# Attention and two feed-forward layers on one core: where the second layer's weights are converted

## The chip, the cores and the metric

The kernel runs on one core of a Trainium2 chip. The core has TensorE (PE) for matrix products, VectorE (DVE), ScalarE (ACT) and GpSimd (POOL) for elementwise work, and SyncE (SP), whose queue issues all transfers (DMA) of this kernel. Each engine works through its own instructions in order and waits for semaphores of the others. The metric is the device time of one execution in microseconds (us).

## The reference

```python
# q, k, v: 4 batches x 8 heads x 768 positions x 64, fp32
scores = scale * q @ k^T                     # keep: first 4 positions, or the last 128
a = softmax(where(keep, scores, -1e9)); x = a @ v        # -> x: 3072 tokens x 512
h = x @ w1_in                                # 512 -> 2048
x = (h - tanh(h)) @ w1_out                   # 2048 -> 512
out = relu(x @ w2_in) ** 2 @ w2_out          # 512 -> 2048 -> 512
```

Weights are given in 64-bit floats, x in fp32, and the result is fp32.

## The kernel before

Each fp32 number is split into a high and a low part, and each product is three matmuls (high by high, high by low, low by high). `split` does it: ACT makes the high part (L150), DVE or POOL the low part (L151). Weights come as 64-bit floats and are made single on the chip by `to_single`: one instruction of ACT (L132) and three of DVE (L133 to L135).

The first layer goes in 8 tiles of 384 tokens, and each tile in 16 chunks `fc` of 128 hidden units: first product (L455), tanh (L466), difference (L467), split into `gs` or a spare buffer (L150, L151), and second product (L487) into `acc`, one chunk late, in tile 7 two chunks late. Between the pieces of a chunk a hook is called at four places, q = 0 to 3; it puts in the attention of the next tile. Tile 7 has no next one. There the second layer is opened: x is loaded (L681), four sums (L690) and seven splits of it go to POOL, and DVE and ACT turn its w_in into seven operands (L648, L657, L658).

The second layer goes in 6 tiles of 512 tokens with 8 groups each. A group is two hidden chunks, as seven block products in place of eight: `first` does four of them, `rest` three, and between them stands the second product (L756) of the group before, in two halves. w_out is fetched (L618) chunk by chunk out of DRAM, from where the kernel put it, converted, earlier.

That earlier conversion is the matter here. It goes in 64 half chunks, 32 of w_in and 32 of w_out, all through one buffer `wos` (`bufs=1`): load (L583), conversion with a `w_bit` buffer, and then for w_in a store of `w_bit` (L590), for w_out a split back into `wos` by ACT and POOL, and a store of that (L595). The next load must wait for that store. Before, `early_step` is called in every place q = 3 of tiles 1 to 6: in tiles 1 and 2 each call converts a half chunk of w_in and then loads the next one; in tiles 3 to 6 a call at an even place loads a half chunk of w_out and the call at the odd place after it converts it.

The order of PE is written by hand. The order of the other engines and of SP comes out of a scheduler, from priorities, its own estimates and `issue_after` (not before this instruction), and each then works in that order.

Of the kernel before, what the change touches and what calls it, by code (L numbers as in the profile page):

```python
# [13 lines left out]
I32 = mybir.dt.int32  # L14
# [5 lines left out]
P = 128  # L20
B, H, S, D = 4, 8, 768, 64
DM, DFF = 512, 2048
KC = DM // P
FC = DFF // P
T = 384
NT = B * S // T
# [13 lines left out]
NP = 7  # L40
# [87 lines left out]
def to_single(c, raw, w):  # L128

    nc = c.nc  # L130
    lo, hi = raw[:, :, 0], raw[:, :, 1]
    nc.scalar.activation(hi.bitcast(F32), hi.bitcast(F32), AF.Copy, scale=2.0 ** -112)  # L132
    nc.vector.tensor_scalar(w, hi, 3, None, ALU.logical_shift_left)  # L133
    nc.vector.scalar_tensor_tensor(w, lo, 29, w, ALU.logical_shift_right, ALU.bitwise_or)  # L134
    nc.vector.scalar_tensor_tensor(w, hi, -2147483648, w, ALU.bitwise_and, ALU.bitwise_or)  # L135


def convert(c, raw, dst, lo_eng):

    w = c.sb.tile([P, DM], I32, tag="w_bit", name="w_bit", bufs=3)[:, : raw.shape[1]]  # L140
    to_single(c, raw, w)
    dst = dst()
    split(c, dst, w.bitcast(F32), lo_eng)
    return dst


def split(c, dst, src, lo_eng):

    nc = c.nc
    nc.scalar.activation(dst[:, 0, :], src, AF.Copy)  # L150
    lo_eng.tensor_tensor(dst[:, 1, :], src, dst[:, 0, :].bitcast(F32), ALU.subtract)  # L151


class Weights:


    def __init__(self, c, w_in, w_out):
        self.c, self.src, self.t = c, (w_in, w_out), [[None] * FC, [None] * FC]
# [8 lines left out]
    def convert(self, i, fc):  # L167
        self.t[i][fc] = convert(self.c, self.t[i][fc], lambda: slot(self.c, ("wi", "wo")[i], fc, F32R),
                                (self.c.nc.vector, self.c.nc.gpsimd)[i])
# [378 lines left out]
def pools(c, es):  # L548
    tc = c.tc
    c.wp = es.enter_context(tc.tile_pool(name="wp", bufs=1))  # L550
    c.xp = es.enter_context(tc.tile_pool(name="xp", bufs=1))
    c.fp = es.enter_context(tc.tile_pool(name="fp", bufs=1))
    c.ps = es.enter_context(tc.tile_pool(name="ps", bufs=1, space=PSUM))
    c.sb_es = es.enter_context(ExitStack())
    c.sb = c.sb_es.enter_context(tc.tile_pool(name="sb", bufs=1))
    c.spare = lambda fc: c.sb.tile([P, 3 * WN], F32R, tag="p", name="p", bufs=2)


# [7 lines left out]
class Second:  # L566


    def __init__(self, c):
        self.c = c  # L570
        self.slots = {}
        self.w = {}
        self.wo = {}
        self.x = {}
        self.xs = {}
        self.f = {}

# [5 lines left out]

    def convert_in(self, i):
        c, (fc, h) = self.c, divmod(i, 2)
        w = c.sb.tile([P, DM], I32, tag="w_bit", name="w_bit", bufs=3)[:, : DM // 2]
        to_single(c, self.early, w)
        c.nc.sync.dma_start(c.wi2[fc, :, ts(h, DM // 2)], w.bitcast(F32))  # L590

    def convert_out(self, i):
        c, (fc, h) = self.c, divmod(i, 2)
        t = convert(c, self.early, lambda: c.fp.tile([P, 2, DM // 2], F32R, tag="wos", name="wos", bufs=1), c.nc.gpsimd)
        c.nc.sync.dma_start(c.wo2[fc, :, :, ts(h, DM // 2)], t.bitcast(F32))  # L595

    def early_step(self, step):

        c = self.c
        with c.tc.issue_after(c.last_a.ins), c.tc.issue_after(c.last_d.ins):  # L600
            if step < 2 * FC:
                if step == 0:
                    self.load(c.w2_in, 0)
                self.convert_in(step)
                if step + 1 < 2 * FC:
                    self.load(c.w2_in, step + 1)
            elif step % 2 == 0:
                self.load(c.w2_out, step // 2 - FC)
            else:
                self.convert_out(step // 2 - FC)  # L610

    def fetch_out(self, fc):
        c, k = self.c, fc % 4
# [9 lines left out]
    def open(self):  # L623
        c = self.c
        c.l2 = c.sb_es.enter_context(c.tc.tile_pool(name="l2", bufs=1))
        c.spare = lambda fc: c.l2.tile([P, 2 * DM], F32R, tag=f"wos{2 + fc // 2 % 2}", name=f"wos{2 + fc // 2 % 2}", bufs=1)
        self.load_x(0)
        self.load_in(0)
        self.load_in(1)
        self.sum_x(0)  # L630
        for name in ORDER:
            self.split_x(0, name)
# [135 lines left out]
    def run(self, left):  # L768
        nj = B * S // T2
        half = (len(left) + 1) // 2  # L770
        before = left[:half], left[half:]
        for n in range(nj * NG):
            j, g = divmod(n, NG)
            s = self.first(j, g)
            if g == NG - 1 and j + 1 < nj:
                for name in ORDER[:4]:
                    self.split_x(j + 1, name)
            for m in before[0]:
                m()
            self.rest(j, g, s)  # L780
            if g == NG - 1 and j + 1 < nj:
                for name in ORDER[4:]:
                    self.split_x(j + 1, name)
            for m in before[1]:
                m()
            if n + 1 < nj * NG:
                for f in range(2):
                    self.fetch_out(2 * ((n + 1) % NG) + f)
            if j + 1 < nj:
                if g == 2:  # L790
                    self.load_x(j + 1)
                if g == 4:
                    self.sum_x(j + 1)
            before = [lambda j=j, g=g, s=s: self.second(j, g, s, 0)], [lambda j=j, g=g, s=s: self.second(j, g, s, 1)]
        for part in before:
            for m in part:
                m()


def banded(c):  # L800

    nc, tc = c.nc, c.tc
    with ExitStack() as es:
        pools(c, es)
        layers = [Weights(c, c.w1_in, c.w1_out)]
        heads = Heads(c, None)
        second = Second(c)
        loaded = 0

        def next_chunk():  # L810
            nonlocal loaded
            if loaded < 2 * FC:
                layers[0].load(loaded % 2, loaded // 2)
                loaded += 1

        heads.vsink = c.sb.tile([P, H + 1, D], F32, tag="v_k", name="v_k", bufs=1)
        nc.vector.memset(heads.vsink, 0.0)
        c.eps = c.const.tile([P, 1], F32, tag="eps", name="eps")
        nc.vector.memset(c.eps, 1.0e-9)
        for n in range(H):  # L820
            heads.load(n)
            if n == 1:
                nc.sync.dma_start(heads.vsink[:NS, :H, :], c.vs[0, :NS])
            if n in (3, 5, 7):
                next_chunk()
                next_chunk()
        heads.masks = band_masks(c)
        for pos in range(8 * H + OFF):
            heads.tick(pos)
        for fc in range(LEAD):  # L830
            for i in range(2):
                with tc.issue_after(heads.mark[2].ins), tc.issue_after(heads.markd[2].ins):
                    layers[0].convert(i, fc)

        def hook(l, j, fc, q):
            if j == 0 and q % 2 == 0:
                next_chunk()
            if j + 1 < NT:
                heads.tick(64 * (j + 1) + OFF + 4 * fc + q)
            f = fc + LEAD - (q == 1)  # L840
            if j == 0 and q % 2 == 1 and LEAD <= f < FC:
                with tc.issue_after(c.last_a.ins), tc.issue_after(c.last_d.ins), tc.issue_after(c.last_r.ins):
                    layers[0].convert(int(q == 1), f)
            if 1 <= j < NT - 1 and q == 3:
                second.early_step((j - 1) * FC + fc)
            if j == NT - 1:
                if fc == 0 and q == 0:
                    c.sb_es.close()
                    second.open()
                if q == 3:  # L850
                    with tc.issue_after(c.last_a.ins), tc.issue_after(c.last_d.ins):
                        second.before(fc)

        with tc.manual_schedule(engines={mybir.EngineType.PE}):
            second.run(ffn(c, layers, lambda l, j: heads.x[j], hook))
# [133 lines left out]
```

## Time and profile before

| what | value |
|---|---|
| median of 3 runs | 1279.56 us (1279.18 to 1281.78) |
| profiled execution | 1281.62 us, of which the span 1279.4 |
| PE busy | 1241.4 us, 97% of the span |
| PE weight loads | 1160.9 us, 91% |
| DVE busy | 824.8 us, 64% |
| ACT busy | 656.1 us, 51% |
| POOL busy | 356.3 us, 28% |
| mean granted TensorE clock | 0.997 |

The share of an engine is over the whole span; a single tile or group can have another limit. In rows of a timeline the first number is the start in us from the start of the span, the second the duration of the piece, then engine, line, operation, output <- input and number of instructions; in brackets stands how long the engine was idle before, and for what it waited. SPq is the queue of SP, and its rows are the issues of transfers.

### The profile page before, as it was taken

Reading aid. Unit: us, or ns where it says so; the run is one execution under the profiler, and the core shown is the slowest. Engines: PE = TensorE matmul, PEld = TensorE weight load, DVE = VectorE, ACT = ScalarE, POOL = GpSimd, SP = SyncE. Lnnn points to the kernel's source line nnn. Section 1 sums busy time; section 2 is a strip of 40 time slices with the busy share of each in tenths; the row PEclk is TensorE's granted clock in tenths of the full one; section 3 lists DMA queues with packets and bytes.
Section 4 is the critical chain, followed back from the end, with each engine's and each line's share of the span. In section 5 each row is a group of like instructions: output and inputs, shape, how many; then the busy total and the mean of one; then the engine's idle time right before and its main releaser. Section 6 shows DMA issues by size and latency. Waiting matters only on the chain.

```text
span 1279.4 us, 21220 instructions
## 1 busy us (share of the span) xinstructions
PE 1241.4 (97%) x7632; PEld 1160.9 (91%) x7632; DVE 824.8 (64%) x2012; ACT 656.1 (51%) x1714; POOL 356.3 (28%) x349
## 2 busy tenths in 40 slices
PE   7999999999899999999999999999999999999997
PEld 5788899988899999999999998999999999999996
DVE  7899777777776777767775775455464554554543
ACT  7887666756566777766774542232322322323221
POOL 0222323323233343434341402032230320323100
PEclk9999999999999999999999999999999999999999
DMA  9741144443333433333413233343253342533432
GB/s 364 269 169 45 66 132 129 126 129 119 95 119 109 133 114 99 123 106 109 133 50 123 63 113 124 99 142 122 99 165 99 100 165 99 165 101 105 137 103 87
DMA packets 67795, 158.27 MB, mean 124 GB/s; under 512 B 6864, under 2 KB 29392, under 8 KB 67680
## 3 DMA queue, kind: packets, MB, share of 16 engines
q1 hardware_dynamic: 67680, 156.82, 37.3%
q8 instruction: 62, 1.02, 0.3%
q14 instruction: 53, 0.43, 0.1%
HBM read 131.63 MB, written 25.17 MB: 123 GB/s over the span
## 4 chain that ended last, share of the span: by engine, by line
PE 75%; DVE 12%; DMA 6%; ACT 5%; issue 2%; POOL 0%; SPq 0%; ACTq 0%; DVEq 0%; POOLq 0%
PE acc L756 21%; PE acc L487 14%; PE ps_h L455 12%; DMA wos<-in_w_in_dram 5%; PE ps_h L705 5%; PE ps_v L705 5%; PE ps_t L705 5%; PE ps_s L705 3%; DVE w_bit L135 3%; DVE w_bit L134 2%; PE ps_t L322 2%; DVE w_bit L133 1%; PE ps_s L270 1%; DVE gs L151 1%; PE ps_s L271 1%
## 5 line engine op out<-in xcount | busy, mean ns | idle before, releaser
L487 PE MATMUL acc<-gs,wo 128*128 128x384 f32 x1440 | 297.7, 343 | 1.0 <-ACT gs L150 0.6
L455 PE MATMUL ps_h<-x,wi 128*128 128x384 f32 x1392 | 292.7, 345 | 2.9 <-DVE t L467 2.8
L487 PEld LDWEIGHTS acc<-gs,wo 128*128 128x128 f32 x1440 | 246.2, 188 | 3.8 <-ACT gs L150 1.0
L455 PEld LDWEIGHTS ps_h<-x,wi 128*128 128x128 f32 x1392 | 237.0, 189 | 7.5 <-DVE t L467 6.8
L150 ACT ACTIVATE x<-gs 128x256 fp32r<-128x256 f32 x144 | 55.0, 412 | 201.9 <-DVE gs L722 127.4
L756 PE MATMUL acc<-wos,x 128*128 128x512 f32 x576 | 139.5, 391 | 0.0
L151 POOL TENSOR_TENSOR x<-gs,x 128x256 fp32r<-128x256 f32 x48 | 35.7, 743 | 333.0 <-ACT x L150 333.0
L756 PEld LDWEIGHTS acc<-wos,x 128*128 128x128 f32 x576 | 105.2, 188 | 19.9
L467 DVE TENSOR_TENSOR t<-ps_h,t 128x384 f32<-128x384 f32 x116 | 64.6, 557 | 70.3 <-ACT t L466 70.1
L279 ACT ACTIVATE p<-p,nm 128x272 f32<-128x272 f32 (+1 forms) x168 | 83.7, 498 | 25.6 <-DVE nm L272 24.1
L219 POOL TENSOR_TENSOR k_l<-qkv,k_h 128x416 fp32r<-128x416 f32 (+1 forms) x48 | 60.7, 1264 | 114.9 <-ACT k_h L218 114.4
L272 DVE CUSTOM_DVE_ANT_0 p<-ps_s,m 128x272 f32<-128x272 f32 (+1 forms) x168 | 69.7, 415 | 30.2 <-PE ps_s L271 28.6
L151 DVE TENSOR_TENSOR gs<-t,gs 128x384 fp32r<-128x384 f32 x120 | 71.6, 596 | 13.0 <-ACT gs L150 12.8
L150 ACT ACTIVATE gs<-t 128x384 fp32r<-128x384 f32 x120 | 62.8, 523 | 32.8 <-DVE t L467 30.3
L756 PE MATMUL acc<-wo,x 128*128 128x512 f32 x288 | 73.8, 391 | 2.4 <-DMA wo<-wo 2.4
L756 PE MATMUL acc<-wi,x 128*128 128x512 f32 x288 | 73.7, 391 | 0.0
L151 POOL TENSOR_TENSOR wos<-w_bit,wos 128x256 fp32r<-128x256 f32 x32 | 23.6, 739 | 175.2 <-ACT wos L150 72.2
L151 POOL TENSOR_TENSOR xop<-xs,xop 128x512 fp32r<-128x512 f32 x42 | 58.1, 1414 | 35.6 <-ACT xop L150 35.6
L307 ACT ACTIVATE pt<-ps_t 128x384 fp32r<-128x384 f32 (+1 forms) x112 | 51.7, 462 | 29.0 <-PE ps_t L322 28.3
L292 DVE TENSOR_SCALAR p<-p,sm 128x128 f32<-128x128 f32 (+1 forms) x144 | 64.5, 473 | 1.9
L756 PEld LDWEIGHTS acc<-wo,x 128*128 128x128 f32 x288 | 52.5, 188 | 12.5 <-issue 2.6
L151 DVE TENSOR_TENSOR x<-gs,x 128x256 fp32r<-128x256 f32 x96 | 46.9, 529 | 22.9 <-ACT x L150 22.9
(187 smaller groups left out, 2512.4 us busy)
## 6 DMA issues: line engine op xcount, KB each, us to landing
wos<-wo SPq DMA_DIRECT2D x48, 512.0 KB, 4.0
qkv<-in_a_dram SPq DMA_DIRECT2D x32, 608.0 KB, 4.2
wi<-wo SPq DMA_DIRECT2D x24, 512.0 KB, 3.2
wo<-wo SPq DMA_DIRECT2D x24, 512.0 KB, 4.3
qkv<-in_a_dram SPq DMA_DIRECT2D x24, 504.0 KB, 3.9
wi<-in_w_in_dram SPq DMA_DIRECT2D x16, 512.0 KB, 9.5
wo<-in_w_out_dram SPq DMA_DIRECT2D x16, 512.0 KB, 8.8
wos<-in_w_in_dram SPq DMA_DIRECT2D x32, 256.0 KB, 2.9
```

The lines of the kernel that those rows point to most:

```text
L150: nc.scalar.activation(dst[:, 0, :], src, AF.Copy)
L151: lo_eng.tensor_tensor(dst[:, 1, :], src, dst[:, 0, :].bitcast(F32), ALU.subtract)
L219: nc.gpsimd.tensor_tensor(s.kl[:, :nk], s.k[:, :nk], s.kh[:, :nk].bitcast(F32), ALU.subtract)
L272: c.last_r = nc.vector.tensor_tensor_reduce(out=s.p[:, u, :w], in0=sc[:, :w], in1=self.masks[kind], op0=ALU.add, op1=ALU.min, scale=-SCALE ...
L279: self.mark[n] = nc.scalar.activation(s.p[:, u, :w], s.p[:, u, :w], AF.Exp, bias=s.nm[:, u : u + 1], scale=-1.0, accum_out=s.sm[:, u : u + 1])
L292: nc.vector.tensor_scalar(s.p[:, u, :w], s.p[:, u, :w], s.sm[:, u : u + 1], None, ALU.mult)
L307: nc.scalar.activation(hi, src, AF.Copy)
L455: nc.tensor.matmul(h[:, :T], w[:, a, kc, :], x[kc][:, b, :], start=(kc == 0 and i == 0), stop=(kc == KC - 1 and i == 2))
L467: c.last_d = nc.vector.tensor_tensor(t, h[:, :T], t, ALU.subtract)
L487: nc.tensor.matmul(acc[m][:, :T], w[:, a, ts(m, P)], gs[:, b, :], **st)
L705: self.c.nc.tensor.matmul(bank, w[:, a, kc, :], x[:, b, kc, :], start=start and kc == 0 and i == 0, stop=kc == 1 and i == 2, skip_group_ch ...
L756: nc.tensor.matmul(self.acc[2 * th + m], gs[:, b, ts(m, P)], w[:, a, :], start=(g == 0 and q == 0 and i == 0), stop=(g == NG - 1 and q == ...
```

## The change

One half chunk is converted at every second place of tiles 1 to 7: `early_load` at the even places, `early_convert` at the odd ones, 8 in a tile. w_in takes tiles 1 to 4, w_out half chunks 0 to 23 tiles 5 to 7; the last eight go into the loop over the groups of the second layer's first tile, up to two calls in a group. The `w_bit` buffer comes from the second layer's `xs` buffers once that layer is opened. In the second layer the next tile's x is loaded after group 4 instead of 2, and its sums are made after group 5 instead of 4. Everything else is the same.

```diff
 def convert(c, raw, dst, lo_eng):
-    w = c.sb.tile([P, DM], I32, tag="w_bit", name="w_bit", bufs=3)[:, : raw.shape[1]]
+    w = c.bits()[:, : raw.shape[1]]
...
+    c.bits = lambda: c.sb.tile([P, DM], I32, tag="w_bit", name="w_bit", bufs=3)
...
-    def early_step(self, step):
...
+    def early_load(self):
+        if self.done < 4 * FC:
+            self.load(*((self.c.w2_in, self.done) if self.done < 2 * FC else (self.c.w2_out, self.done - 2 * FC)))
+    def early_convert(self):
+        if self.done < 4 * FC:
+            if self.done < 2 * FC:
+                self.convert_in(self.done)
             else:
-                self.convert_out(step // 2 - FC)
+                self.convert_out(self.done - 2 * FC)
+            self.done += 1
...
     def open(self):
+        c.bits = lambda: c.l2.tile([P, DM], I32, tag="xs", name="xs", bufs=NP)
...
+            if j == 0:
+                for _ in range(2):
+                    self.early_load()
+                    self.early_convert()
             if j + 1 < nj:
-                if g == 2:
+                if g == 4:
                     self.load_x(j + 1)
-                if g == 4:
+                if g == 5:
                     self.sum_x(j + 1)
...
-            if 1 <= j < NT - 1 and q == 3:
-                second.early_step((j - 1) * FC + fc)
+            if j >= 1 and q == 3:
+                with tc.issue_after(c.last_a.ins), tc.issue_after(c.last_d.ins):
+                    (second.early_convert if fc % 2 else second.early_load)()
```

The lines of the changed kernel stand up to five further down: L583 is L585, L595 is L597, L648 is L649, L657 and L658 are L658 and L659, L681 is L682, L690 is L691.

ACT in tile 7, from the split of chunk 3 (`wos3`) to that of chunk 4 (`gs`); `wo1`, `wo0` and `wi1` take operands of the second layer. Before:

```order
L150 ACTIVATE wos3_8748<-t_8747 128x384
L657 ACTIVATE wo1_8774<-x_8603 128x256
L657 ACTIVATE wo0_8768<-xs_8759 128x2x256
L657 ACTIVATE wi1_8771<-xs_8760 128x2x256
L466 ACTIVATE t_8800<-ps_h_8787 128x384
L150 ACTIVATE gs_8801<-t_8800 128x384
L466 ACTIVATE t_8831<-ps_s_8818 128x384
```

And the same place of the changed kernel, where `wos_8563` is a half chunk just loaded and `wos_8601` its high part:

```order
L150 ACTIVATE wos3_8585<-t_8584 128x384
L658 ACTIVATE wo1_8620<-x_8427 128x256
L466 ACTIVATE t_8646<-ps_h_8633 128x384
L132 ACTIVATE wos_8563<-wos_8563 128x256
L150 ACTIVATE gs_8647<-t_8646 128x384
L658 ACTIVATE wo0_8614<-xs_8605 128x2x256
L150 ACTIVATE wos_8601<-xs_8596 128x256
L658 ACTIVATE wi1_8617<-xs_8606 128x2x256
L466 ACTIVATE t_8679<-ps_s_8666 128x384
```

The first step of a conversion now stands ahead of chunk 4's split, two operands of the second layer stand behind it, and the half chunk's own split is between them.

SP at the end of tile 7: `wi15`, `wo15` and `wos2` are the places of w_out chunks 0, 1 and 2 for the second layer, `xs` loads of the x of its second tile, `o` results of the first layer. Before:

```order
L618 DMA wi15_9295<-wo2_63 128x1024
L681 DMA xs_9615<-x2_61 128x2x256
L618 DMA wos2_9411<-wo2_63 128x1024
L681 DMA xs_9617<-x2_61 128x2x256
L681 DMA xs_9619<-x2_61 128x2x256
L681 DMA xs_9621<-x2_61 128x2x256
L505 DMA x2_61<-o_9399 128x384
L505 DMA x2_61<-o_9402 128x384
L618 DMA wo15_9297<-wo2_63 128x1024
```

And the changed kernel there, where `wos_9095`, `wos_9130` and `wos_9186` are half chunks in their one buffer:

```order
L618 DMA wi15_9207<-wo2_63 128x1024
L597 DMA wo2_63<-wos_9095 256x1x256
L618 DMA wos2_9323<-wo2_63 128x1024
L585 DMA wos_9130<-in_w2_out_dram 128x512
L597 DMA wo2_63<-wos_9186 256x1x256
L505 DMA x2_61<-o_9311 128x384
L618 DMA wo15_9209<-wo2_63 128x1024
```

The fetch of chunk 1 stands behind the last load and store of tile 7, and the loads of the next x are gone from here.

SP again, at the last groups of the second layer's first tile, in the changed kernel: the load and the store of the last half chunks, the fetches of w_out chunks 14 and 15 (`wos2`, `wos3`) and the x loads of the second tile.

```order
L585 DMA wos_9691<-in_w2_out_dram 128x512
L597 DMA wo2_63<-wos_9698 256x1x256
L618 DMA wos2_10018<-wo2_63 128x1024
L585 DMA wos_9702<-in_w2_out_dram 128x512
L682 DMA xs_9811<-x2_61 128x2x256
L682 DMA xs_9813<-x2_61 128x2x256
L682 DMA xs_9815<-x2_61 128x2x256
L597 DMA wo2_63<-wos_9709 256x1x256
L682 DMA xs_9817<-x2_61 128x2x256
L618 DMA wos3_10020<-wo2_63 128x1024
```

In the kernel before, this stretch of SP holds fetches of w_out alone; the x loads stand at the end of tile 7, as above.

## Rows read from the trace of the kernel before

**Rows 1.** Busy time by stretch, tiles 1, 2, 3, 4 and 7 of layer 1.

```profile
core 0: us, PE busy (x) PEld busy (x) DVE busy (x) ACT busy (x) POOL busy (x), PEclk, DMA share, GB/s
162.50:252.30 89.80, 87.70 (x540) 83.91 (x539) 68.35 (x195) 58.86 (x164) 27.68 (x28) 1.00 0.43 131
252.30:355.00 102.70, 93.52 (x575) 88.23 (x575) 75.54 (x196) 63.70 (x170) 31.14 (x30) 1.00 0.38 117
355.00:439.30 84.30, 84.30 (x540) 84.26 (x539) 59.34 (x170) 58.33 (x166) 32.33 (x35) 1.00 0.34 112
439.30:528.10 88.80, 88.80 (x576) 88.74 (x575) 63.74 (x172) 63.26 (x169) 35.84 (x38) 1.00 0.34 110
699.70:770.20 70.50, 69.52 (x410) 68.32 (x409) 52.44 (x106) 36.49 (x74) 18.79 (x15) 1.00 0.32 100
```

**Rows 2.** Waits of PE's weight loads, tiles 1 and 2: us in total, times, longest.

```profile
PEld ps_s L270 <- DVE nm L272: 9.5, 13, 1.9
PEld ps_v L377 <- DVE pts L309: 4.0, 3, 2.5
```

**Rows 3.** Waits of ACT, tiles 1 and 2.

```profile
ACT wos L132 <- DMA wos<-in_w_in_dram: 28.9, 31, 2.4
```

**Rows 4.** Timeline: a half chunk of w_out in tile 4, the last one before tile 7.

```profile
454.28 0.43 ACT L132 ACTIVATE wos<-wos 128x256 f32<-128x256 f32 x1
...
458.74 0.52 SPq L595 DMA_DIRECT2D wo<-wos  x1
...
461.30 0.33 SPq L583 DMA_DIRECT2D wos<-in_w_out_dram  x1
...
693.08 0.43 ACT L132 ACTIVATE wos<-wos 128x256 f32<-128x256 f32 x1
...
695.91 0.74 POOL L151 TENSOR_TENSOR wos<-w_bit,wos 128x256 fp32r<-128x256 f32 x1 [3.83 <-ACT wos L150]
...
696.67 0.53 SPq L595 DMA_DIRECT2D wo<-wos  x1
```

**Rows 5.** DMA issues: count, KB each, median us from issue to landing.

```profile
wo<-wo SPq DMA_DIRECT2D x24, 512.0 KB, 4.3
...
wos<-in_w_out_dram SPq DMA_DIRECT2D x32, 256.0 KB, 2.7
...
xs<-x SPq DMA_DIRECT2D x24, 256.0 KB, 5.5
```

**Rows 6.** Timeline of tile 7: POOL's x splits, DVE, and PE at chunks 4 and 8.

```profile
707.13 9.79 POOL L151 TENSOR_TENSOR xop<-xs,xop 128x512 fp32r<-128x512 f32 x7
...
715.70 1.50 DVE L648 TENSOR_TENSOR xs<-x,xs 128x256 f32<-128x256 f32 x1
...
721.35 2.19 PE L487 MATMUL acc<-gs,wo 128*128 128x384 f32 x11 [0.15 <-DVE gs L151]
...
722.35 0.42 DVE L648 TENSOR_TENSOR xs<-x,xs 128x256 f32<-128x256 f32 x1
...
737.94 2.24 PE L487 MATMUL acc<-gs,wo 128*128 128x384 f32 x12
```

**Rows 7.** Timeline: PE at the second layer's first accumulation.

```profile
775.42 1.61 PE L756 MATMUL acc<-wo,x 128*128 128x512 f32 x6 [2.39 <-DMA wo<-wo]
```

**Rows 8.** Timeline: end of the second layer's first tile, first group of the next.

```profile
834.56 1.68 SPq L618 DMA_DIRECT2D wos<-wo  x2
...
837.68 5.25 POOL L151 TENSOR_TENSOR xop<-xs,xop 128x512 fp32r<-128x512 f32 x4 [7.13 <-ACT xop L150]
...
848.40 0.88 PE L705 MATMUL ps_v<-xop,wo 128*128 128x256 f32 x6
```

**Rows 9.** Busy time by stretch (columns of rows 1): after the start, and around rows 7.

```profile
36.00:46.00 10.00, 7.68 (x38) 5.60 (x37) 7.94 (x19) 9.63 (x26) 3.56 (x4) 0.90 0.73 274
46.00:50.00 4.00, 4.00 (x21) 3.82 (x20) 2.87 (x6) 2.62 (x9) 0.68 (x1) 0.82 0.00 0
772.90:783.30 10.40, 8.01 (x46) 6.94 (x45) 4.81 (x12) 1.95 (x5) 0.74 (x1) 1.00 0.39 134
```

More of the change, by code (lines that the diff above doesn't have):

```diff
@@ L576, in __init__ @@
         self.f = {}
+        self.done = 0
     def load(self, src, i):
@@ L587, in convert_in @@
         c, (fc, h) = self.c, divmod(i, 2)
-        w = c.sb.tile([P, DM], I32, tag="w_bit", name="w_bit", bufs=3)[:, : DM // 2]
+        w = c.bits()[:, : DM // 2]
         to_single(c, self.early, w)
@@ L595, in convert_out @@
         c.nc.sync.dma_start(c.wo2[fc, :, :, ts(h, DM // 2)], t.bitcast(F32))
-    def early_step(self, step):
[L599 to L608, printed above, removed]
-            else:
-                self.convert_out(step // 2 - FC)
+    def early_load(self):
[5 more added lines that the diff above has]
+                self.convert_in(self.done)
+            else:
+                self.convert_out(self.done - 2 * FC)
+            self.done += 1
     def fetch_out(self, fc):
```

## The prediction

> **What bounds the kernel now.** Four views were read, in this order: the page's totals, the stretches by tile, the waits in the stretches that stand out, and the rows around every place where a converted half chunk goes in the changed kernel. The totals say that TensorE (PE) is busy nearly all of the span, so only time in which PE waits can be won, and any new wait of PE is lost at full price. The stretches by tile [rows 1] run from one tile's first result copy to the next. Tiles 1 and 3 hold the same matmuls (x540), and so do tiles 2 and 4 (x575 and x576), yet tile 1 takes 89.8 us against 84.3 and tile 2 takes 102.7 against 88.8. Tiles 3 and 4 have no idle PE at all. What tiles 1 and 2 have more of is conversions: a w_in half chunk at each of 16 places, where tiles 3 and 4 convert a w_out half chunk at every second place. The waits of tiles 1 and 2 [rows 2] are for the scores' maximum and for copies out of PSUM, both on VectorE (DVE). Behind them stands ScalarE (ACT): in 31 of the 32 places its L132 waits for the load of the half chunk, 28.9 us in all [rows 3], because that load is issued only when the half chunk before it has left the one buffer. ACT works in order, so softmax and tanh steps stand behind L132.
>
> From tile 7 on the same view shows 70.5 us with 1 us of idle PE; no half chunk is converted there, but POOL has seven splits of the second layer's x and DVE splits its w_in.
>
> **Tiles 1 to 6: gain.** The change halves the conversions of tiles 1 and 2 (8 each instead of 16), and issues each load a place ahead of its conversion. I take tile 1 to become as long as tile 3, and tile 2 as tile 4: 89.8 - 84.3 = 5.5 and 102.7 - 88.8 = 13.9, so -19.4 [rows 1]. What is hidden there afterwards (three DVE instructions, one of ACT) is hidden in tiles 3 and 4 by the same work already, and a w_in half chunk has no split on top. The gain could be less if some of the extra time belongs to attention itself; -10 is the other bound, about half. Tiles 3 to 6 stay at 8 half chunks each: nothing.
>
> **Tile 7: loss.** Here each half chunk goes through one buffer: load, L132 on ACT, three DVE instructions, a split on ACT and POOL, store, and only then the next load. In tile 4 [rows 4] that took 454.28 to 458.74 = 4.46 from L132 to store, then 2.56 to the next load; the last half chunk before tile 7 took 693.08 to 696.67 = 3.6 [rows 4]. With 2.7 for a load to land [rows 5] the cycle is 3.6 + 2.56 + 2.7 = 8.9 to 9.7 us; I take 9.1. PE does four chunks in 16.6 us (721.35 to 737.94, [rows 6]), 8.3 for two, so the buffer is slower than the places that it serves.
>
> First harm: POOL's split of tile 7's first half chunk stands behind seven xop splits, which end at 707.13 + 9.79 = 716.92 [rows 6]. With 0.74 for such a split [rows 4] it ends at 717.7; the next load can go at 717.7 + 2.56 = 720.2, and lands at 722.9. In the order of the changed kernel the L132 for that half chunk stands on ACT immediately ahead of the hi split of chunk 4, and on DVE three conversions and five w_in instructions stand ahead of chunk 4's lo split. L132 ends at 722.9 + 0.43 = 723.4; nine DVE instructions at 0.42 [rows 6] give 727.2. PE needed that lo split at 721.35 [rows 6]: 5.9 us late. Two conversions later L132 again stands ahead of a split: 727.2 + 2 x 9.1 = 745.4 against 737.94 [rows 6], 7.4 late. After that the order has L132 behind the split, and the delay only stays.
>
> Second harm: the fetch of w_out chunk 1 for the second layer's first accumulation. In before it was what PE waited for (2.39 us, [rows 7]), and it landed at 775.42. Now SP has load and store of tile 7's last half chunk ahead of it. The second conversion's L132 starts at 722.9; the eighth is six cycles on, 722.9 + 6 x 9.1 = 777.5; store after 4.0, then 0.5 for its issue, and 4.3 for the fetch [rows 5]: 786.3. Against 775.42 that is +10.9, and it contains the delays before it, since PE waits there anyway. Bounds: 7.4 (only the first harm), and +14.5 with the cycle at 9.7. I take +10.9.
>
> **Boundary of the second layer's tiles 0 and 1: loss.** The last eight half chunks go about one to a group. Within the groups before the last I cost them at nothing: L132 waits for loads there too, but PE uses what ACT, DVE and POOL make of a group only in the group after it; without that cover each would add its conversion, up to 4.5 us as in tile 4 [rows 4]. The end is different. In before the next tile's x loads and POOL sums were done by the end of tile 7; now the loads stand in SP's queue behind the load of the last half chunk, which stands behind the fetch of chunk 14, issued at 834.56 [rows 8]. So: that load at 834.9, landed at 837.6, split and store by about 841.6; the x loads at 835.3 to 836.3, landing 5.5 later [rows 5] at 841.8. Then POOL needs three sums, two splits, one sum, and two splits before the fourth product of the next tile can run: eight instructions at 1.31 (5.25 for four, [rows 8]) to 1.40 (9.79 for seven, [rows 6]); the second, since sums are among them: 841.8 + 11.2 = 853.0. PE wanted it at 848.40 [rows 8]: +4.6. Bounds 3.9 (all at 1.31) and 6.1 (a start 1.5 us later). Later tiles have a whole group between their loads and their sums, without half chunks: nothing.
>
> **Clock.** After idle stretches the granted clock fell in this trace: 0.90 over 10 us in which PE was busy for 7.68, and 0.82 over the 4 after that [rows 9], which cost 10 x 0.10 + 4 x 0.18 = 1.7 us. Around the wait of 2.39 us before the second layer's accumulation it stayed 1.00 [rows 9]. The changed kernel has three gaps of 3 to 5 us, at chunk 4, at the fetch and at the boundary. I count one of them with a fall: +1.7; bounds 0 and 5.1.
>
> The Trainium skill, "TensorE: Matmul & The Clock Gate", section "HAM oscillation — how this bites in real kernels", says that waits for transfers between bursts of matmuls bring the slow clock back each time; by it all three gaps would pay. The trace shows both outcomes [rows 9], and no run so far shows gaps of this size in the middle of dense work.
>
> **Sum.** -19.4 + 10.9 + 4.6 + 1.7 = -2.2 us, against the profiled execution's 1281.62 (span 1279.4 and 2.2 around it). That execution is 2.06 above the median of the runs, 1279.56, so I subtract from the median: 1277.4, rounded to 1277.5.
>
> **Rivals.**
> - *The blocks are covered* (faster). If the cycle in tile 7 is short, or L132's landing is earlier than I reckon, the two chunks by which the second matmul lags absorb the delay, and only some DVE work of tile 7 shows. For it: DVE is idle for 18 of tile 7's 70.5 us [rows 1]. Against: SP's order, which puts the fetch behind the store whatever DVE does. Price: -19.4 and some 3 left over: 1263. If only one of the two losses comes, it is 1267 to 1273.
> - *The one buffer's cycle* (slower). In tile 7 DVE's instructions took up to 1.50 us beside POOL's splits, 0.42 after them [rows 6], and ACT and DVE carry work that tile 4 doesn't have. Each 0.1 us on the cycle costs six times that at the fetch. At 10.3 instead of 9.1 it is +7.2: 1284.7. It decides from a cycle of about 9.9 on: (1282.1 - 1277.5) / 6 = 0.77 more. For it: the long DVE rows; against: POOL has nothing after its seven splits, and ends before most of the eight half chunks.
> - *The waits of tiles 1 and 2 are not the conversions'* (slower). Then they lose only half, -9.7, and the losses stand: 1287. Against: tiles 3 and 4 do the same attention with no idle PE [rows 1].
>
> **How the numbers follow.** A change of 0.2%, 2.6 us, is about what a measurement of this kernel can tell from none: 1277.0 to 1282.1. The forecast, a gain of tiles 1 and 2 that tile 7 and the boundary eat up, gets 0.40; its own range is 1273 to 1282 (0.16 below 1277.0, 0.24 within). The covered case gets 0.18 and one loss alone 0.10, both faster. The longer cycle gets 0.24 (0.20 slower, 0.04 within), the third rival 0.08. Faster: 0.16 + 0.18 + 0.10 = 0.44; same 0.28; slower 0.28. The range of 8 in 10 reaches from the covered case, 1262, to the longer cycle with part of the clock, 1286.
>
> **What would show it.** Tiles 1 and 2 at about 84 and 89 us, without PE waits for L272 and L309: the gain. ACT's L132 waiting for its load in tile 7 and PE waiting at chunks 4 and 8 for DVE's L151, then up to 5 us for the fetch of chunk 1: the first loss. PE waiting for POOL's xop splits in the second layer's ninth group: the second. The clock below 1.00 right after those gaps: the last term. The prediction is wrong if tile 7 keeps its 70.5 us, or if tile 2 stays over 95.

## The result, and the profile after

| | before | changed |
|---|---|---|
| median (6 runs each, side by side) | 1281.22 us | 1297.61 us |
| ratio | | 1.0121, interval 1.0109 to 1.0134 |
| span of the profiled execution | 1279.4 us | 1295.4 us |
| mean granted TensorE clock | 0.997 | 0.989 |

The change made the kernel slower by 1.2%, where a gain of 2 us was forecast. The two traces can be laid side by side at four places: the copy that ends a tile (L501), the first accumulation of the second layer (775.42 before, [rows 7]), the fourth product of its second tile (848.40, [rows 8]) and the end.

| stretch | before | after | difference | forecast |
|---|---|---|---|---|
| start to tile 1 | 162.5 | 161.6 | -0.9 | 0 |
| tile 1 | 89.8 | 84.3 | -5.5 | -5.5 |
| tile 2 | 102.7 | 88.8 | -13.9 | -13.9 |
| tiles 3 to 6 | 344.7 | 344.7 | 0 | 0 |
| start of tile 7 to the first accumulation | 75.7 | 96.4 | +20.7 | +10.9 |
| from there to the fourth product of the second tile | 73.0 | 85.4 | +12.4 | +4.6 |
| from there to the end | 431.0 | 434.2 | +3.2 | (clock 1.7) |

Busy time by stretch of the changed kernel, columns as in [rows 1]: tiles 1, 2, 3 and 7, which answer to those rows; then four short stretches of tile 7 and two at the second tile of layer 2.

```profile
161.60:245.90 84.30, 84.30 (x540) 84.26 (x539) 59.24 (x171) 55.05 (x158) 26.45 (x28) 1.00 0.33 103
245.90:334.70 88.80, 88.80 (x576) 88.73 (x575) 63.75 (x172) 59.94 (x161) 29.93 (x30) 1.00 0.32 99
334.70:419.00 84.30, 84.30 (x540) 84.27 (x539) 59.25 (x171) 54.99 (x158) 26.40 (x28) 1.00 0.33 103
679.40:770.90 91.50, 77.55 (x413) 74.18 (x412) 58.44 (x126) 40.98 (x91) 28.91 (x20) 0.93 0.34 107
...
688.50:694.50 6.00, 2.85 (x15) 2.27 (x14) 5.28 (x6) 2.81 (x7) 6.00 (x6) 0.98 0.00 0
694.50:698.00 3.50, 3.50 (x12) 3.50 (x13) 3.50 (x4) 1.21 (x3) 3.50 (x3) 0.54 0.00 0
703.00:711.00 8.00, 5.11 (x20) 4.53 (x19) 6.39 (x15) 4.51 (x10) 2.17 (x1) 0.81 0.27 74
755.00:766.00 11.00, 7.39 (x36) 7.18 (x35) 7.06 (x17) 4.19 (x10) 1.83 (x2) 0.69 0.51 167
847.00:857.00 10.00, 4.41 (x20) 3.38 (x19) 5.79 (x10) 5.46 (x13) 8.19 (x7) 0.88 0.56 189
857.00:867.00 10.00, 8.86 (x38) 7.76 (x38) 3.74 (x6) 1.78 (x4) 8.76 (x8) 0.60 0.14 58
```

Tiles 1 and 2 have no idle PE any more and are as long as tiles 3 and 4: the gain came to a tenth. Tile 7 is 21 us longer. PE idles there for 14 us (91.50 - 77.55) where it idled for 1, and most of the rest stands in the column PEclk: its matmuls are the same, but they take 77.55 us in place of 69.52, because after the waits the engine ran at the lower level (6.1 of these 8 us are found row by row below). In the second short stretch the granted clock is 0.54, which is close to 1.2 GHz all through; PE had been busy for 2.85 of the 6 us before it.

How the half chunks went through the one buffer in tile 7 shows in ACT's L132, by start, duration and what it waited for; first of the eight, then five of the others.

```profile
688.68 0.42 ACT L132 ACTIVATE wos<-wos 128x256 f32<-128x256 f32 x1
...
703.72 0.44 ACT L132 ACTIVATE wos<-wos 128x256 f32<-128x256 f32 x1 [7.73 <-DMA wos<-in_w_out_dram]
...
714.27 0.43 ACT L132 ACTIVATE wos<-wos 128x256 f32<-128x256 f32 x1 [4.70 <-DMA wos<-in_w_out_dram]
...
724.68 0.44 ACT L132 ACTIVATE wos<-wos 128x256 f32<-128x256 f32 x1 [0.62 <-DMA wos<-in_w_out_dram]
...
737.44 0.44 ACT L132 ACTIVATE wos<-wos 128x256 f32<-128x256 f32 x1 [3.71 <-DMA wos<-in_w_out_dram]
...
766.43 0.44 ACT L132 ACTIVATE wos<-wos 128x256 f32<-128x256 f32 x1 [1.56 <-DMA wos<-in_w_out_dram]
```

From the second on each L132 stands waiting for its load. From the second to the eighth it is 62.7 us, six cycles of 10.45, where the forecast had 9.1. One of the cycles in full (second to third half chunk), on DVE, POOL and SP:

```profile
704.19 0.29 DVE L133 TENSOR_SCALAR xs<-wos 128x256 int32<-128x256 int32 x1 [5.32 <-ACT wos L132]
...
705.41 0.42 DVE L135 SCALAR_TENSOR_TENSOR xs<-wos,xs 128x256 int32<-128x256 int32 x1
...
706.59 2.17 POOL L151 TENSOR_TENSOR wos<-xs,wos 128x256 fp32r<-128x256 f32 x1 [8.46 <-ACT wos L150]
707.01 0.55 DVE L151 TENSOR_TENSOR gs<-t,gs 128x384 fp32r<-128x384 f32 x1
...
708.08 0.55 DVE L467 TENSOR_TENSOR t<-ps_s,t 128x384 f32<-128x384 f32 x1
...
708.79 0.52 SPq L597 DMA_DIRECT2D wo<-wos  x1
...
711.31 0.33 SPq L585 DMA_DIRECT2D wos<-in_w_out_dram  x1
```

L132 to store is 5.07 us, store to load 2.52, load to L132 2.96. In this cycle the first part is the one that grew most: POOL's split takes 2.17 us where [rows 4] has 0.74, for the fourth half chunk even 3.19, and DVE puts steps of the w_in operands between L133 and L135. Over the six cycles L132 to store takes 28.5 us, where 9.1 a cycle leaves 23.0 for it, and load to L132 18.8, where six times 2.7 is 16.2: 5.5 and 2.6 us of the excess. POOL's split ends at 708.76, 0.68 us after the start of L467 (708.08), which takes one input out of PSUM; the DVE instructions that ran since the split began have both inputs in SBUF. Seven of tile 7's eight splits end 0.67 to 0.69 us after the start of such an instruction (L467, once L739). Chunk 4's low split (707.01) stands behind all of DVE's steps, as forecast. What PE sees of it, the waits of PE in tile 7 and then from there to 900 us (us in total, times, longest):

```profile
PE acc L487 <- DVE gs L151: 6.2, 4, 2.6
PE ps_v L706 <- DVE t L467: 3.6, 1, 3.6
PE acc L487 <- ACT gs L150: 2.0, 2, 1.7
PE acc L487 <- ACT wos L150: 1.8, 2, 1.0
...
PE ps_h L706 <- POOL xop L151: 4.3, 1, 4.3
PE acc L757 <- DMA wo<-wo: 1.5, 1, 1.5
PE ps_h L706 <- ACT xop L150: 1.3, 1, 1.3
PE ps_t L706 <- POOL xop L151: 1.1, 1, 1.1
```

Of the first four the three on L487 are the waits for splits at chunks 2, 4, 6, 8, 11 and 13, and the one on L706 is for the PSUM bank of chunk 15's first product. The wait for the fetch answers to [rows 7], those for `xop` to [rows 8]. The places of PE that matter most, in order of time:

```profile
692.42 0.45 PE L487 MATMUL acc<-gs,wo 128*128 128x384 f32 x1 [1.68 <-ACT gs L150]
694.34 3.70 PE L487 MATMUL acc<-gs,wo 128*128 128x384 f32 x11 [1.47 <-DVE gs L151]
...
707.62 3.64 PE L487 MATMUL acc<-gs,wo 128*128 128x384 f32 x11 [2.56 <-DVE gs L151]
...
760.55 1.65 PE L706 MATMUL ps_v<-xop,wo 128*128 128x256 f32 x6 [3.61 <-DVE t L467]
762.00 4.04 PE L487 MATMUL acc<-gs,wo 128*128 128x384 f32 x12
...
775.83 1.63 PE L757 MATMUL acc<-wo,x 128*128 128x512 f32 x6 [1.53 <-DMA wo<-wo]
...
855.90 1.44 PE L706 MATMUL ps_h<-xop,wi 128*128 128x256 f32 x5 [4.31 <-POOL xop L151]
857.14 1.48 PE L706 MATMUL ps_s<-xop,wo 128*128 128x256 f32 x6
...
862.49 4.07 PE L757 MATMUL acc<-wos,x 128*128 128x512 f32 x12
```

Eleven matmuls of chunk 4 took 2.19 us before [rows 6]; here the eleven after the wait take 3.64. Taking from each such row what the same matmuls take elsewhere gives 1.5 at 694.34, 1.4 at 707.62, 0.6 at chunk 11, 2.6 at 760.55 and 762.00, and 3.8 between 855.90 and 866.40: 9.9 us by the clock, where the forecast had 1.7.

### The profile page after: what moved, and what is told of

The parts are those of the page before. It is cut to its first block, busy times and chain, and to the rows that moved or that the text cites. A ratio compares the mean times of both kernels' runs of the same rounds, so it can differ in the third digit from the quotient of the medians.

```text
span 1295.4 us, 21207 instructions
## 1 busy us (share of the span) xinstructions
PE 1245.1 (96%) x7632; PEld 1169.6 (90%) x7632; DVE 819.0 (63%) x2012; ACT 651.2 (50%) x1714; POOL 360.3 (28%) x349
## 3 DMA queue, kind: packets, MB, share of 16 engines
q8 instruction: 62, 1.02, 0.3%
## 4 chain that ended last, share of the span: by engine, by line
PE 77%; DVE 8%; DMA 5%; ACT 3%; POOL 3%; issue 2%; SPq 0%; ACTq 0%; POOLq 0%; DVEq 0%
PE acc L757 18%; PE acc L487 16%; PE ps_h L455 16%; PE ps_v L706 5%; PE ps_t L706 5%; PE ps_h L706 5%; DMA wos<-in_w_out_dram 3%; PE ps_t L322 2%; PE ps_s L706 2%; DVE w_bit L134 2%; DVE w_bit L135 2%; DMA wo<-wos 2%; PE ps_s L271 1%; PE ps_s L270 1%; PE ps_v L363 1%
## 5 line engine op out<-in xcount | busy, mean ns | idle before, releaser
L487 PE MATMUL acc<-gs,wo 128*128 128x384 f32 x1440 | 302.8, 348 | 8.2 <-DVE gs L151 6.2
L487 PEld LDWEIGHTS acc<-gs,wo 128*128 128x128 f32 x1440 | 250.5, 191 | 11.9 <-DVE gs L151 7.4
L467 DVE TENSOR_TENSOR t<-ps_h,t 128x384 f32<-128x384 f32 x116 | 64.6, 557 | 68.4 <-ACT t L466 68.4
L309 DVE TENSOR_TENSOR pt<-ps_t,pt 128x384 fp32r<-128x384 f32 x96 | 50.1, 522 | 21.1 <-ACT pt L307 21.1
L757 PEld LDWEIGHTS acc<-wo,x 128*128 128x128 f32 x288 | 52.5, 188 | 11.6 <-issue 1.7
L151 DVE TENSOR_TENSOR x<-gs,x 128x256 fp32r<-128x256 f32 x96 | 46.8, 529 | 24.3 <-ACT x L150 24.1
```

Source lines behind the costliest of these rows:

```text
L467: c.last_d = nc.vector.tensor_tensor(t, h[:, :T], t, ALU.subtract)
L487: nc.tensor.matmul(acc[m][:, :T], w[:, a, ts(m, P)], gs[:, b, :], **st)
L757: nc.tensor.matmul(self.acc[2 * th + m], gs[:, b, ts(m, P)], w[:, a, :], start=(g == 0 and q == 0 and i == 0), stop=(g == NG - 1 and q == ...
```

## The experiments

After the two traces the theory was: the conversions of tile 7 and of the second layer's first tile cost PE time because each half chunk passes through one buffer, and the cycle of that buffer is longer than the places it serves. The rivals: the conversions' own work on ACT, DVE and POOL, beside tile 7's work on w_in; and the second layer's later x loads. All ratios are to the kernel before.

| run | what | median us | ratio (interval) |
|---|---|---|---|
| e1_none_late | no half chunks in tile 7 and layer 2 (16 left out) | 1262.4 | 0.9863 (0.9846 to 0.9879) |
| e2_tile7_alone | the last 8 left out | 1281.0 | 1.0009 (0.9996 to 1.0022) |
| e3_layer2_alone | tile 7's 8 left out | 1264.0 | 0.9872 (0.9856 to 0.9888) |
| e4_before_prefetch | before, loads a place ahead | 1276.9 | 0.9974 (0.9964 to 0.9984) |
| e5_raw_buffer | changed, own buffer for loads | 1269.1 | 0.9915 (0.9890 to 0.9940) |
| e6_x_loads_early | changed, x loads as before | 1296.3 | 1.0115 (1.0090 to 1.0141) |
| e7_skip_first | changed, 7 in tile 7, 9 after it | 1290.1 | 1.0072 (1.0046 to 1.0099) |
| e8_spread_early | none in tile 7, 56 in tiles 1 to 6 | 1271.5 | 0.9929 (0.9907 to 0.9952) |
| e9_late_eight | e5, last 8 tied to groups 1 to 4 | 1264.2 | 0.9876 (0.9857 to 0.9894) |
| e10_late_nine | e9, 7 in tile 7, 9 after it | 1267.1 | 0.9900 (0.9880 to 0.9920) |
| e11_split_on_dve | changed, low half on DVE | 1280.7 | 1.0007 (0.9993 to 1.0020) |

**Where the loss sits: e1, e2, e3.** The hook's condition is cut for tile 7, or the loop over groups, or the first of the two with the count moved on:

```diff
-            if j >= 1 and q == 3:
+            if 1 <= j < NT - 1 and q == 3:          # e1, e3
-            if j == 0:
+            if j < 0:                               # e1, e2: loop of layer 2
+            if j == NT - 1 and fc == 0 and q == 3:  # e3
+                second.done = 3 * FC + FC // 2
```

> The changed kernel with conversions in tiles 1 to 6 alone; the last 16 half chunks of w_out are left out, and the fetches take chunks that are there instead, the same bytes. If all that was lost comes from the conversions in tile 7 and in the second layer's first tile, this keeps the 20.3 us won up to the start of tile 7 and loses nothing: tile 7 back at 70.5 us, about 1281.2 - 20.3 = 1261, ratio 0.984. Rival: the later loads and sums of the second layer's x (groups 4 and 5 in place of 2 and 4) cost the wait at its second tile by themselves: then 4 to 10 us remain there, 1265 to 1271.

> The changed kernel without the eight conversions of the second layer's first tile (left out; fetches take chunks that are there). If tile 7 and the second layer lose independently, the 20.7 us from the start of tile 7 to the first accumulation stay and the rest goes: 1261 + 20.7 = 1282, ratio 1.000. If the delays feed each other (a delayed last half chunk of tile 7 holds up the fetches), less than 18 stay: under 1279.

> The changed kernel without the eight conversions of tile 7 (left out; fetches take chunks that are there); those of the second layer's first tile are done. If the two lose independently: 1261 + 15.3 = 1276, ratio 0.996, with PE waiting for POOL's xop splits at the second tile for 5 us or more. If the boundary was late only because everything before it was late, 1261 to 1266.

e1 came out as expected: tiles 1 to 6 bring the gain, tile 7 is back at 70.6 us, and the later x loads alone cost nothing. From e1 to e2 it is 18.5 us, a little under the 20.7 of the trace: e2 came out as its first case. e3 was the surprise, its second case: the last eight alone cost 1.5 us, within the intervals, and not 15. Their first load goes out at the start of tile 7, where the buffer is free, and the last one 52.5 us after the first accumulation, where the changed kernel has 67.1. Both together cost 33 us by the ratios and 35 by the medians, so 13 to 15 us are neither the one nor the other: they come when both are there and tile 7's half chunks push the last eight later.

**Where the gain came from: e4.** The kernel before, with loads into the `w_bit` buffers, so that one is under way while another is converted:

```diff
-        t = c.fp.tile([P, 2, DM // 2], I32, tag="wos", name="wos", bufs=1).rearrange("p a c -> p (a c)")
+        t = c.sb.tile([P, DM], I32, tag="w_bit", name="w_bit", bufs=3)
...
+                    self.load(c.w2_in, step + 1)
                 self.convert_in(step)
-                    self.load(c.w2_in, step + 1)
```

> The kernel before, with each half chunk loaded into a w_bit buffer in place of the one wos buffer, so that the load of a half chunk is issued a place ahead of its conversion; 16 conversions in tile 1 and in tile 2 as before, all done before tile 7. If the waits of tiles 1 and 2 came from ACT standing at L132 for its load, these go and tiles 1 and 2 fall to 84 to 87 and 89 to 93: 1262 to 1268, ratio 0.985 to 0.990. If they come from the work of 16 conversions on DVE and ACT, at most half goes: 1271 or more, ratio over 0.992.

ACT's wait for loads at L132 in tiles 1 and 2 is gone, 0.7 us in place of 28.9 [rows 3]:

```profile
ACT w_bit L132 <- DMA w_bit<-in_w_in_dram: 0.7, 1, 0.7
```

Tiles 1 and 2 are 85.0 and 94.9 us long, 4.8 and 7.8 shorter. Tile 1 still holds 16 conversions, so there the load's wait was 4.8 of the 5.5 us. Tile 2 holds only 12 now, and tile 3 has 11 where it had 8 and takes 91.2 us in place of 84.3. So of the 19.4 us at most 12.6 are the load's wait, and 5.7 are left when tile 3 is counted. The whole gains 3 us, which falls under the expectation's second case, by its time; the sum of the first missed tile 3. Why tile 2 falls behind even without the wait is not shown.

**The cycle of the buffer: e5 and e11.** In e5 the load from tile 7 on goes into a buffer of its own, so it waits for DVE's L135 of the half chunk before and no longer for that one's split and store. In e11 the buffer stays, and DVE makes the low half.

```diff
+        c.raw = lambda: c.l2.tile([P, DM], I32, tag="raw", name="raw", bufs=1)    # e5, in open()
-        t = c.fp.tile([P, 2, DM // 2], I32, tag="wos", ...)
+        t = c.raw()
...
-        t = convert(c, self.early, lambda: ..., c.nc.gpsimd)
+        t = convert(c, self.early, lambda: ..., c.lo)      # e11: c.lo = c.nc.vector from open() on
```

> The changed kernel with a buffer of its own for the loaded half chunk from tile 7 on, so that a load waits for the conversion before it and no longer for that one's split and store; nothing is left out. If the cycle of the one buffer (10 to 15 us a half chunk in the trace after) is what made tile 7 long, the waits at chunks 4 and 8 and at the end go, the collision of the first half chunk with POOL's xop splits stays: tile 7 at 75 to 79 us in place of 91.5, and with the last eight done earlier also less at the second tile: 1268 to 1275 in all, ratio 0.990 to 0.996. If the work of the conversions on ACT, DVE and POOL beside the w_in operands is the cause, tile 7 stays at 86 or more: 1288 to 1298.

> The changed kernel with the one buffer kept, and the low half of a half chunk's split made by DVE instead of POOL from tile 7 on; nothing is left out. POOL took 2.2 and 3.2 us for such a split in tile 7 where it took 0.74 in tile 4; DVE would take about 0.5. If that slow split is a main part of the cycle, each of the eight gets 1 to 2.4 us shorter, and 8 to 14 us come back: 1283 to 1289. If the cycle is set by load, store and DVE's own queue, a DVE with more in it gives nothing: 1294 to 1300.

Tile 7 of e5, and then its PE waits from the start of tile 7 to the first accumulation:

```profile
680.20:752.60 72.40, 70.04 (x415) 68.90 (x414) 61.17 (x132) 42.68 (x93) 29.61 (x21) 1.00 0.44 143
```

```profile
692.23 0.44 PE L487 MATMUL acc<-gs,wo 128*128 128x384 f32 x1 [0.72 <-ACT gs L150]
694.16 2.18 PE L487 MATMUL acc<-gs,wo 128*128 128x384 f32 x11 [1.49 <-DVE gs L151]
758.74 1.62 PE L759 MATMUL acc<-wo,x 128*128 128x512 f32 x3 [3.87 <-DMA wo<-wo]
```

With the same eight conversions in it and one of the last eight besides, and DVE even busier than in the changed kernel (61.17 against 58.44), tile 7 takes 72.4 us. Three of POOL's splits still take 2.83 to 3.17 us there, but no load waits for them. The waits at chunks 4 to 15 are gone and so is the one for POOL's xop splits at the second tile. That settles it for the cycle: the work of the conversions finds room in tile 7, the wait for the buffer doesn't. It was expected a little longer (75 to 79).

In e11 tile 7 takes 77.3 us, with a cycle of 9.6 (700.20 to 757.58 for six), by ACT's second and eighth L132:

```profile
700.20 0.43 ACT L132 ACTIVATE wos<-wos 128x256 f32<-128x256 f32 x1 [1.58 <-DMA wos<-in_w_out_dram]
...
757.58 0.42 ACT L132 ACTIVATE wos<-wos 128x256 f32<-128x256 f32 x1
```

Against the changed kernel that is 15 us by the ratios and 17 by the spans, more than the 8 to 14 expected. L132 to store takes 3.9 us in the mean, 4.75 in the changed kernel. So POOL's split was a main part of what made the cycle long, although it is one instruction of 0.74 us by [rows 4]. But e11 moves two things more. The first split no longer stands behind POOL's xop splits, so the second L132 comes 20.7 us after the start of the tile and not 24.3; and SP's order came out otherwise, with the fetch of w_out chunk 1 ahead of the eighth half chunk's store. What each of the three gave of the 15 to 17 us is not shown.

**The collision at the start: e7 and e10.** The first conversion of tile 7 goes, and the loop of the second layer takes one more; e10 is the same on e9.

```diff
-            if j >= 1 and q == 3:
+            if 1 <= j < NT and q == 3 and (j < NT - 1 or fc >= 2):
```

> The changed kernel with tile 7's first conversion moved to the end: seven in tile 7, from its chunk 2 on, nine in the second layer's first tile; nothing is left out. If the collision of the first half chunk with POOL's seven xop splits costs what PE shows at chunk 2 (3.2 us idle, 1.5 by the clock) and starts the chain late, tile 7 falls by 5 to 10 us to 82 to 86: 1287 to 1292. If the cycle alone sets tile 7, it falls by no more than 3, and the ninth half chunk makes the second tile later still: 1294 to 1302.

> e9_late_eight with tile 7's first conversion, the one beside POOL's seven xop splits, moved to the end as well (seven in tile 7, nine in the second layer's first tile); nothing is left out. If the 2.2 us that PE waits at tile 7's chunk 2 in e5_raw_buffer come from DVE's conversion steps slowed beside those splits, they go: 1263 to 1266, 2 us under e9_late_eight. Rival: the ninth half chunk brings the wait at the second layer's second tile back: not under e9_late_eight.

e7 is 6 to 8 us under the changed kernel and its tile 7 is 83.2 us long, the numbers of its first case, but hardly for the reason given there: the chain does not start earlier (second L132 25.9 us after the start of the tile), it is one half chunk shorter, and its cycle is 9.2 us, with POOL's splits at 0.74 to 1.11 beside other DVE instructions than before. e10 shows that the collision itself gives nothing back: PE's wait of 2.4 us at chunk 2 becomes 1.3 at chunk 3 and 0.9 at chunk 4. No wait comes at the second layer's second tile, but a new one near the end of its first, where ACT stands at L132 for 7.3 us for the ninth half chunk:

```profile
814.13 0.98 PE L708 MATMUL ps_h<-xop,wo 128*128 128x256 f32 x6 [2.11 <-ACT wi L721]
```

It is not faster than e9.

**The x loads: e6.** Groups 2 and 4 in place of 4 and 5:

```diff
-                if g == 4:
+                if g == 2:
                     self.load_x(j + 1)
-                if g == 5:
+                if g == 4:
                     self.sum_x(j + 1)
```

> The changed kernel with the second layer's x loaded after group 2 and summed after group 4, as before; nothing is left out. If the loss at the second layer's second tile came from x loads queued on SP behind the last half chunks, 5 to 10 us of it go: 1287 to 1292. If it came from POOL, whose sums still stand behind a split that follows the late groups, it stays: 1295 to 1299.

Nothing came back, as in the second case, but PE's longest wait at the second tile is now another, 3.7 us for the fetch of the last w_out chunk, which needs the last half chunk's store:

```profile
861.54 5.28 PE L757 MATMUL acc<-wos,x 128*128 128x512 f32 x12 [3.74 <-DMA wos<-wo]
```

When the eight are late, one or the other waits for them.

**Better versions: e8 and e9.** e8 converts w_in at two of three places of tiles 1 to 3 and w_out at every second place of tiles 4 to 6:

```diff
+            p = (j - 1) * FC + fc
+            if 0 <= p < 3 * FC and q == 3:
...
+                    if p % 3 < 2:
+                        second.early_convert()
+                        second.early_load()
...
```

> All 64 half chunks without any in tile 7: w_in at two of three places of tiles 1 to 3 (32), w_out at every second place of tiles 4 to 6 (24), the last eight in the second layer's first tile as in e3_layer2_alone, which cost 1.5 us there; nothing is left out. Between 8 conversions a tile (no waits) and 16 (5.5 and 13.9 us in tiles 1 and 2), 10 or 11 should cost 1 to 3 us a tile: 1264 + 3 to 9 = 1267 to 1273, ratio 0.990 to 0.995. Rival: any two conversions in neighbouring places wait for the load as before, and half of the old loss comes in three tiles: 1276 or more.

Tiles 1 to 3 are 86.1, 91.2 and 85.4 us long, 5.3 us over 84.3, 88.8 and 84.3 together. e9 is e5, with the last eight behind an instruction of `first` in groups 1 to 4, so that the fetch of w_out chunk 1 is no longer behind a store of theirs on SP:

```diff
-            if j == 0:
-                for _ in range(2):
+            if j == 0 and g >= 1:
+                with self.c.tc.issue_after(s.mark.ins):
+                    for _ in range(2):
...
```

> e5_raw_buffer with the last eight half chunks tied to the second layer's groups 1 to 4, two in a group, so that the fetch of w_out chunk 1 stands ahead of their loads and stores on SP; nothing is left out. If the wait of 3.9 us for that fetch in e5_raw_buffer, and the slow clock after it, came from the queue on SP, both go back to the 2.4 us of the kernel before: 1.5 idle and about 1.5 of clock less, 1265 to 1268, ratio 0.988 to 0.990. Rival: two half chunks in a group delay the group's own results and PE waits there: 1269 to 1275.

The wait for the fetch is 1.65 us in place of 3.87:

```profile
757.11 1.61 PE L759 MATMUL acc<-wo,x 128*128 128x512 f32 x6 [1.65 <-DMA wo<-wo]
```

The whole came out a little under the 1265 to 1268 expected. e9 is the fastest with nothing left out: 1.2% under the kernel before, and 2 us from e1, which leaves a quarter of the conversions out. Both its steps, the load's own buffer and the place of the last eight, were taken from the waits above.

## Why the prediction was wrong

By the spans the forecast is missed by 18.2 us: 9.8 from the start of tile 7 to the first accumulation, 7.8 from there to the second tile, 1.5 after it, less 0.9 won before tile 1. The mechanism of the losses was the forecast's; the size of the buffer's cycle, and what hangs on it, was not.

- **Tiles 1 to 6** were right, to 0.1 us in each tile: a tile with eight conversions was there to be read [rows 1]. The reason given, ACT at L132, holds for tile 1 (4.8 of 5.5 us in e4); for both tiles it is at most 12.6 of 19.4, and the rest stays open.
- **Tile 7 fails at its cycle of 9.1 us**, made up from rows of tile 4 and tile 6 [rows 4]. It measured 10.45, and over six cycles that is 8.1 of the 9.8 us by which the stretch was missed. The start was 1.1 us late: the second L132 came 24.3 us after the start of the tile, forecast 23.2. In the cycle, L132 to store was the part most under-sized, 3.84 us of the 9.1 against 4.75 measured; the landing of the load, 2.7 against 3.1, is a third of the miss. The cycle was my rival on the slower side, priced at 10.3, with a chance of 0.24; what I held against it was that POOL has nothing to do after its seven splits. But idle before the split is not alone during it: three of the eight splits took 2.2 to 3.2 us and the others 1.05 to 1.42, while DVE ran instructions on two SBUF inputs next to them. e11, which takes POOL out of the cycle, has 3.9 us from L132 to store. The Trainium skill, "SBUF — State Buffer", section "Who interferes with whom", says that a DVE instruction with two SBUF inputs contends with a GpSimd instruction that reads SBUF, and that the later one is held. The durations agree, 0.74 alone and up to 3.19; that POOL stayed held over several short DVE instructions in a row is seen here and not said there.
- **The first half chunk** was counted only as the start of the chain. Its own conversion steps stand ahead of chunk 2 on ACT and DVE, and beside the xop splits DVE needed 3.1 us for them (0.73, 1.38 and 1.02). PE lost 3.2 us in waits and 1.5 by the clock there. e10 says that it can't be had back just by leaving that place free.
- **The boundary fails by the same buffer.** I had the last eight go with PE's groups; from 774.25 on their loads went out one buffer cycle after another, 9.8 us each, with POOL's splits back at 0.74. I had the last load behind the fetch of chunk 14 alone, at 59.5 us after the first accumulation; it went at 67.1, because the store of the half chunk before it had come only 2.8 us earlier. POOL's sums began 8.1 us later than forecast for that. e3 shows the same eight at 1.5 us, when tile 7 doesn't hold them up: I added two losses as if they were independent, and the second is mostly a consequence of the first. Within groups 1 to 6, costed at nothing, 3.0 us went too, where L132 waited for its load ahead of the copies that free PSUM; POOL's late start covers them.
- **The clock** cost PE 9.9 us in place of 1.7. Of the three gaps counted, chunk 4 and the boundary paid; at the fetch, 1.5 us, the matmuls after it took 1.63 us against 1.61 [rows 7]. Three more paid that I didn't have: chunk 2, chunk 11 (0.6 us), and the end of tile 7 (3.6 us for chunk 15's PSUM bank). The wait of 1.81 us at chunk 8 did not: its eleven matmuls took 2.20 us. By the rule cited from the Trainium skill in the prediction all three counted gaps would pay; the trace agrees for two, and the third was shorter than reckoned. The 9.9 us are not all in the total. The first 6.1 lie ahead of the first accumulation, where PE waits for the fetch all the same, and the half chunks' chain in front of that fetch waits for loads and not for PE; that they were covered is argued from the trace, and no run shows it.

The 1.5 us that the clock leaves of the last stretch lie behind the last matmul: the span ends 6.7 us after it before and 8.2 us after it in the changed kernel, and in the thirteen traces this end is 6.4 to 8.2 us long.

## What to carry to other kernels

A buffer that is loaded, worked on and stored sets a cycle, and work that is moved onto it is worth reading as that cycle against the spacing of its places, with the durations of the new neighbourhood and not of the old. Where the cycle is the longer one, each engine that waits for it in order passes the wait on to all that stands behind, and the delay grows with every pass; a second buffer for the load takes it away even if no engine gets less to do. Losses in sequence are not to be added as independent: try the second one without the first.

## What the runs showed of the hardware

- A POOL subtraction of 128x256 took 0.74 us alone and 1.05 to 3.19 beside DVE instructions with two inputs in SBUF; the eight in tile 7 were all over 1 us. Held over up to six such DVE instructions, it ended 0.67 to 0.69 us after the start of the first one with an input out of PSUM (seven of the eight in the changed kernel, and the three long ones of tile 7 in e5). DVE's L134 took 1.38 us in place of 0.42 beside POOL's xop splits.
- Nearly the same two waits at chunk 2 were paid for in one run and not in another: after 0.94 and 1.49 us eleven matmuls took 3.09 us in e9, after 0.72 and 1.49 us they took 2.18 in e5. So it was in two runs more: 3.24 in e11 after 0.94 and 1.48, 2.19 in e6 after 0.59 and 1.49.
